# Two raw V buffers and three transposed buffers, another attention order, and another tail in a one-core attention and soft-MoE kernel

## The chip, the cores and the metric

The kernel runs on one core of a Trainium2 chip. The metric is the device time of one execution in microseconds (us); the time given for a kernel is the median of several runs. Engine names are those of the profile: PE (matrix multiply), DVE (VectorE), ACT (ScalarE), POOL (GpSimd) and SP (here only an issuer of transfers).

## What is computed

Four batches of eight heads, 768 tokens, head size 64: attention to the last 96 tokens and to 8 global keys, with a linear bias by distance. Its output, as 3072 tokens of 512 values, goes through a soft mixture of 8 experts with 4 slots each. All is float32.

```python
scores = 1.0 / np.sqrt(D) * np.matmul(q, k.transpose(0, 1, 3, 2)) + bias     # bias = -slope(head) * distance
scores = np.where(is_global | is_local, scores, -1000000000.0)
a = np.exp(scores - np.max(scores, axis=-1, keepdims=True))
attn_out = np.matmul(a / (np.sum(a, axis=-1, keepdims=True) + 1e-09), v)
x = np.ascontiguousarray(attn_out.transpose(0, 2, 1, 3)).reshape(B * S, H * D)
logits = x @ phi
d = np.exp(logits - logits.max(0, keepdims=True)); d /= d.sum(0, keepdims=True) + 1e-09
slot_input = (d.T @ x).reshape(E, S_per_e, D)
for e in range(E):
    slot_out[e] = np.maximum(slot_input[e] @ w1[e], 0.0) @ w2[e]             # w1 512x1024, w2 1024x512
c = np.exp(logits - logits.max(1, keepdims=True)); c /= c.sum(1, keepdims=True) + 1e-09
return c @ slot_out.reshape(n_slots, D)
```

## The kernel before

**The order is written out by hand.** `ORDER` (line 58) is a list of some 800 steps such as `('v_lo', 8)` or `('proj', 2, 0, 0)`. The loop at L1069 calls the function of each step (table `steps`, L1055 to L1067), and each function appends its instructions to the engines it names. An engine runs its own instructions strictly in that order and waits where an operand is not there; so the list decides on every engine, and on the transfer queue of SP, what stands behind what. Nothing reorders it.

**Attention.** The work is cut in 16 units, a unit being one batch and a pair of heads. Unit u takes `load_qk` and `load_v` (SP, L421 to L425), `scores` (PE, L556), `biased` (DVE, L565: bias added, running maximum), `max_t`/`max_r`, `exponential` (ACT, L581), `w_hi` (ACT, L584: the float16 upper part of the weights), `w_lo` (L591: the rest, six parts for a unit, on POOL, or on DVE as `w_lo_dve`), `v_hi` (POOL, L524) or `v_hi_act` (ACT, L527) and `v_lo` (DVE, L534), which split the raw V in the same way, `values` (PE, L608), `ev_sums`/`ev_recs`/`ev_mul` (DVE, L621 to L633: the division by the sum). Then `tr` (PE, L645) transposes the outcome into a buffer `xt0` or `xt1`, copied there by `tr_copy` (ACT, L650) or `tr_copy_dve` (DVE, L654), and `logits` (PE, L675) multiplies it by phi. After every fourth unit `logits_all` (DVE, L692) closes a batch. The raw V of all units but a few early ones goes through one buffer `vt`: `load_v` of a unit can only be executed when `v_lo` of the one before has read it.

**Memory for weights.** The weights are 64 units of 0.5 MB. 52 of them have a place in the tile `mem` (`HELD`), whose end is at first taken by the attention's buffers (`BUFFERS`); `ld` (L415, SP) loads them in pairs (`PAIRS`) or singly as places come free. The other 12 (`late`, L419) overwrite units that the first expert layer has used up.

**The tail.** After the last unit, a chain over the softmax of the experts ends in `dispatch`, `add` (L769), `slots` (L853); `hid` (L877, PE) is the first expert layer in 8 blocks of 16 matmuls, `relu`/`relu_dve` (L882, L885) its activation, `htp`/`htc` (L890) transposes it, `proj` (L904, PE) is the second layer for four column blocks n, `osc`, `spread` (L913) and `sot` rearrange it, and `comb(n, b)` (L965, PE) gives the output of block n for batches b and b+1 in four banks. `outc`/`outl` (DVE L789, ACT L792) copy these out, and `out` (`out_dma`, L975) has SP issue the transfer to memory. The softmax over slots that `comb` needs is made by `cmax`, `csub`, `cexp`, `csum`, `crec`, `cmul` (L926 to L942), batch by batch.

**The flag.** The fast path holds only for inputs within certain limits. `chk_*` steps gather the evidence, `set_flag` (L1009) turns it into a number and `write_flag` (L1012) stores it; L1076 loads it on every engine, L1077 branches over the general path that stands behind it in the program, and then the engines meet at the end of the program (L1288). In `ORDER` `write_flag` stands behind the last copies, and the loads of L1076 behind the last `out`.

Of the kernel before, what the change touches and what calls it, by code (L numbers as in the profile page):

```python
# [26 lines left out]
NJ = 7  # L27
# [25 lines left out]
PAIRS = 12  # L53
SPLIT = (40, 48)
LATE_AT = (0, 2, 4, 6, 16, 18, 20, 22, 1, 3, 5, 7)
BUFFERS = (("tab0", TABW), ("tab1", TABW), ("raw0", S + KW), ("tab2", TABW), ("raw1", S + KW), ("tab3", TABW), ("tb1", 2 * TW), ("tb2", 2 * TW),
           ("v0", 904), ("vt", NJ * 2 * D), ("xn2", XH), ("tb0", 2 * TW), ("ph1", PW), ("ph0", PW), ("v1", 904), ("xt0", S), ("xt1", S), ("xn0", XH), ("xn1", XH))
# [255 lines left out]
def tile_attention_moe(ctx: ExitStack, tc: tile.TileContext, qk, v, phi, w1, w2, nn, out):  # L313
# [46 lines left out]
    by_head = "p (j i d) -> p j i d"  # L360
    first = 20 * UNIT
    early_q = {2: mem[:, first:first + S + KW], 3: mem[:, first + S + KW:first + 2 * (S + KW)]}
    first += 2 * (S + KW)
    early_v = {1: mem[:, 19 * UNIT:19 * UNIT + VC], 2: mem[:, first:first + VC], 3: mem[:, first + VC:first + 2 * VC]}

    def rqs(u):
        return early_q.get(u, rq[u % 2])

    def vraws(u):
        return early_v.get(u, buf("vt")).rearrange(by_head, j=NJ, i=2)  # L370

    vhi = [buf(f"v{i}", VH).bitcast(F16).rearrange(by_head, j=NJ, i=2) for i in range(2)]
    vlo = [buf(f"v{i}", VV)[:, VH:VV].bitcast(F16).rearrange(by_head, j=NJ, i=2) for i in range(2)]
    tabs = [buf(f"tab{p}").bitcast(BF16).rearrange("p (i c) -> p i c", i=2) for p in range(NP)]
    tbuf = [buf(f"tb{k}").rearrange("p (i c) -> p i c", i=2) for k in range(3)]
    PH = PW // 2
    phi_ = [buf(f"ph{i}", PH).bitcast(F16) for i in range(2)]
    plo_ = [buf(f"ph{i}")[:, PH:2 * PH].bitcast(F16) for i in range(2)]
    xnb = [buf(f"xn{k}")[0:KB].rearrange("p (t f) -> p t f", t=NJ) for k in range(3)]
    xtb = [buf("xt0"), buf("xt1")]  # L380
    table_space = mem[:, area["xn0"][0]:area["xn1"][1]]


# [264 lines left out]
    def tr_copy(u, k):  # L648
        a, n = ((0, 4 * KB), (4 * KB, S - 4 * KB))[k]
        nc.scalar.copy(out=xtb[u % 2][:, a:a + n], in_=ms.pop((u, k))[:, 0:n])  # L650

    def tr_copy_dve(u, k):
        a, n = ((0, 4 * KB), (4 * KB, S - 4 * KB))[k]
        nc.vector.tensor_copy(out=xtb[u % 2][:, a:a + n], in_=ms.pop((u, k))[:, 0:n])  # L654
# [17 lines left out]
    def logits_of(u, k):  # L672
        for s in range(4):
            n = min(SW, S - SW * s)
            nc.tensor.matmul(out=ms[u][32 * s:32 * s + 32, 0:n], lhsT=phis[:, units[u - k][1], :], rhs=xtb[(u - k) % 2][:, SW * s:SW * s + n],  # L675
                             start=(k == 1), stop=(k == 0), skip_group_check=True)
# [296 lines left out]
    def out_dma(n, b, s):  # L973
        o = obs[n, b, s]
        nc.sync.dma_start(out=out_rows(out, n, b)[:, OUT_COLS[s]:OUT_COLS[s] + o.shape[1]], in_=o)  # L975
# [76 lines left out]
    def table_pair(p):  # L1052
# [19 lines left out]
    last_banks.close()
# [219 lines left out]
```

## Time and profile before

| | |
|---|---|
| runs | 193.59, 194.54, 196.99 us; median 194.54 us |
| profiled execution | 192.0 us, of which the profile's span is 190.1 us |
| PE, DVE, ACT, POOL busy in the span | 172.3, 143.1, 124.7, 100.4 us |
| data moved | 61.43 MB at a mean of 323 GB/s |
| attention, until the last `ev_mul` | to 127.9 us |
| chain from there to the first matmul of `hid` | to 136.45 us |
| `hid` | 136.45 to 150.39 us |
| `htp`, `proj`, `comb` | 150.3 to 181.03 us |
| last copies, last transfers, branch, meeting of the engines | 181.03 to 190.1 us |

A row of the profile gives an engine and line, its operation, the operand written and read, and how often (x). Busy time is time in which an instruction of an engine is executed; idle time is put down to the instruction or transfer that released the engine. A name such as `mem` covers many buffers, since most of them are pieces of that one tile.

### The profile page before, as it was taken

How to read it: one execution, taken by the hardware profiler on the slowest of the kernel's cores; microseconds unless marked ns; L12 is line 12 of the kernel's file. 1: busy time of each engine (PE TensorE's matmuls, PEld its weight loads, DVE VectorE, ACT ScalarE, POOL GpSimd, SP SyncE). 2: the span in 40 equal slices, each digit the busy share in tenths (PEclk: the TensorE clock that was granted, in tenths of full speed). 3: DMA queues.
4: the chain of work that ended last, by engine and by line, in shares of the span. 5: the costliest groups of instructions: out<-in, count | busy, mean ns of one | idle time of the engine just before them, and what ended most of it. 6: DMA issues, size and time to landing. Idle time of an engine off the chain costs nothing. (4 is left out here: it accounts for less than half of the span.)

```text
span 190.1 us, 7005 instructions
## 1 busy us (share of the span) xinstructions
PE 172.3 (91%) x2923; PEld 129.9 (68%) x2923; DVE 143.1 (75%) x396; ACT 124.7 (66%) x163; POOL 100.4 (53%) x139
## 2 busy tenths in 40 slices
PE   8999999999799998999999998899999999899800
PEld 2567898989688786878779896584533477687700
DVE  5899899998979979899999999998910612554230
ACT  3399999997989988989699999934200002124420
POOL 6716978987847779768899867802104010000000
PEclk9999999999999999999999999999999999999995
DMA  6999998988997997988548898999999998567872
GB/s 211 415 420 414 423 410 323 403 295 272 393 390 253 335 393 206 385 320 251 179 154 314 299 326 292 340 337 406 414 400 411 407 400 350 193 228 293 313 280 76
DMA packets 16027, 61.43 MB, mean 323 GB/s; under 512 B 1778, under 2 KB 4082, under 8 KB 14450
## 3 DMA queue, kind: packets, MB, share of 16 engines
q1 hardware_dynamic: 15984, 60.89, 85.9%
q8 instruction: 25, 0.41, 0.9%
q14 instruction: 16, 0.13, 0.2%
q10 hardware_dynamic: 2, 0.00, 0.0%
HBM read 54.59 MB, written 6.29 MB: 320 GB/s over the span
## 5 line engine op out<-in xcount | busy, mean ns | idle before, releaser
L591 POOL TENSOR_TENSOR mem<-mem 128x432 f16<-128x432 f32 x81 | 85.9, 1092 | 24.0 <-ACT mem L584 18.1
L556 PE MATMUL sc<-mem 64*128 64x216 f32 (+2 forms) x448 | 45.6, 338 | 2.6 <-DMA mem<-in_qk_dram 1.4
L581 ACT ACTIVATE mem<-mem,nb 128x1296 f32<-128x1296 f32 x32 | 43.5, 1376 | 1.4 <-DVE rsall L621 0.8
L608 PEld LDWEIGHTS <-mem 128*128 128x128 f16 x1248 | 41.6, 97 | 3.1 <-issue 1.6
L608 PE MATMUL x<-mem 128*128 128x65 f16 (+1 forms) x1248 | 43.3, 193 | 0.3 <-POOL mem L591 0.2
L556 PEld LDWEIGHTS sc<-mem 64*128 64x128 f32 x448 | 37.0, 186 | 9.1 <-DVE mx L565 4.1
L584 ACT CAST mem<-mem 128x1296 f16<-128x1296 f32 x31 | 39.5, 1273 | 4.8 <-PE x L608 4.1
L565 DVE CUSTOM_DVE_ANT_1 mem<-sc,mem,mx 128x864 f32<-128x864 f32 x32 | 35.6, 1111 | 1.3 <-DVE mx L565 0.3
L633 DVE CUSTOM_DVE_ANT_1 mem<-x,rc 120x448 f32<-120x448 f32 x32 | 18.8, 621 | 0.5
L534 DVE SCALAR_TENSOR_TENSOR mem<-mem 128x896 f16<-128x896 f32 x16 | 17.5, 1091 | 2.0 <-POOL mem L524 1.3
L645 PE MATMUL m<-ident,mem 120*128 120x120 f32 x105 | 16.3, 277 | 2.1 <-ACT mem L650 1.0
L904 PE MATMUL x<-mem 128*32 128x128 f32 x512 | 16.9, 275 | 1.2 <-issue 0.9
L565 DVE CUSTOM_DVE_ANT_1 mem<-sc,mem 128x864 f32<-128x864 f32 x16 | 16.8, 1052 | 0.9 <-POOL mem L591 0.8
L904 PEld LDWEIGHTS x<-mem 128*32 128x32 f32 x512 | 13.4, 109 | 4.2 <-issue 2.8
L645 PEld LDWEIGHTS m<-ident,mem 120*128 120x128 f32 x105 | 10.8, 141 | 5.5 <-ACT mem L650 1.6
L789 DVE COPY mem<-l 128x480 f32<-128x480 f32 (+1 forms) x14 | 7.6, 593 | 8.5 <-PE l L965 8.5
L877 PE MATMUL l<-mem,sl 128*32 128x512 f32 x128 | 13.9, 593 | 0.0
L792 ACT COPY mem<-m 128x128 f32<-128x128 f32 (+1 forms) x7 | 1.8, 265 | 17.3 <-PE m L890 12.1
L527 ACT ACTIVATE mem<-mem 128x896 f16<-128x896 f32 x13 | 12.3, 947 | 0.8 <-DMA mem<-in_v_dram 0.7
L792 ACT COPY mem<-l 128x480 f32<-128x480 f32 x12 | 6.3, 563 | 9.4 <-PE l L965 9.4
L650 ACT COPY mem<-m 128x288 f32<-128x288 f32 (+1 forms) x25 | 11.5, 470 | 0.7 <-PE m L645 0.6
L885 DVE TENSOR_SCALAR mem<-l,zr 128x512 f32<-128x512 f32 x4 | 2.8, 748 | 10.3 <-PE l L877 10.3
(164 smaller groups left out, 188.2 us busy)
## 6 DMA issues: line engine op xcount, KB each, us to landing
mem<-in_w_dram SPq DMA_DIRECT2D x38, 512.0 KB, 8.7
mem<-in_qk_dram SPq DMA_DIRECT2D x16, 832.0 KB, 6.4
mem<-in_w_dram SPq DMA_DIRECT2D x12, 1024.0 KB, 8.8
mem<-in_v_dram SPq DMA_DIRECT2D x16, 448.0 KB, 5.4
out_dram<-mem SPq DMA_DIRECT2D x16, 240.0 KB, 2.5
out_dram<-mem SPq DMA_DIRECT2D x8, 288.0 KB, 4.1
mem<-in_w_dram SPq DMA_DIRECT2D x2, 256.0 KB, 7.9
mem<-in_w_dram SPq DMA_DIRECT2D x1, 300.0 KB, 6.3
```

Of the source, the lines that this page charges most:

```text
L527: nc.scalar.activation(out=vhi[u % 2][:, :, :, 0:D], in_=vraws(u), func=AF.Copy, scale=V_SC)
L534: nc.vector.scalar_tensor_tensor(out=vlo[k].rearrange("p j i d -> p (j i) d"), in0=vraws(u).rearrange("p j i d -> p (j i) d"), scalar=V_SC ...
L556: nc.tensor.matmul(out=z[:, i, at:at + n], lhsT=r_[r, KCOL[j]:KCOL[j] + KR], rhs=r_[r, KW + KB * j:KW + KB * j + n], start=True, stop=True)
L565: nc.vector.tensor_tensor_reduce(out=tb(u)[:, :, BW * k:BW * k + BW], in0=sc[(3 * u + k) % 2][:, :, 0:BW], in1=table.unit(u % NP, k), scal ...
L581: nc.scalar.activation(out=t, in_=t, func=AF.Exp, bias=nbs[u], scale=T_SC)
L584: nc.scalar.copy(out=blocks(phi_[i])[:, :, 0:QW], in_=tb(u)[:, i].rearrange("p (s c) -> p s c", c=QW))
L591: (engine or nc.gpsimd).tensor_tensor(out=blocks(plo_[i])[:, c, 0:QW], in0=tb(u)[:, i].rearrange("p (s c) -> p s c", c=QW)[:, c], in1=bloc ...
L608: nc.tensor.matmul(out=x[:, (D + 1) * t:(D + 1) * t + d], lhsT=w[:, c:c + P], rhs=vv[:, j, i, 0:d], start=(z == 0), stop=(z == len(ops) - ...
L633: nc.vector.tensor_tensor_reduce(out=xnb[(u // 2) % 3][:, :, c:c + D], in0=xv[:, i, :, 0:D], in1=rcs.pop((u, i)).unsqueeze(2).to_broadcast ...
L645: nc.tensor.transpose(out=m[:, at:at + KB], in_=xnb[(u // 2) % 3][:, t, P * (p % 2):P * (p % 2) + P], identity=ident[0:KB, 0:KB])
L877: nc.tensor.matmul(out=mo["h", a][n][32 * s:32 * s + 32, :], lhsT=slv(a, c, s), rhs=wu[0, 4 * a + s, c][:, 512 * n:512 * n + 512], start=( ...
L904: nc.tensor.matmul(out=xx[32 * s:32 * s + 32, n % 2, 0:w], lhsT=hts[a][c // 4][:, c % 4, s], rhs=wu[1, 4 * a + s, n][:, w * c:w * c + w], ...
```

## The change

Between the buffers, `vt` becomes `vt0` and `vt1` (chosen by the unit's parity) and `xt0`, `xt1` become `xt0`, `xt1`, `xt2` (chosen by the unit modulo 3). The buffers together grow by 1664 floats per partition (0.85 MB), so they begin at unit 23.8 of `mem` where they began at 25.4; `PAIRS` goes from 12 to 11, and two half loads (`SPLIT`) go. A step `out_act` is added, which is `out` issued by ACT, and `ORDER` is written anew.

```diff
-PAIRS = 12
-SPLIT = (40, 48)
+PAIRS = 11
+SPLIT = ()
...
-           ("v0", 904), ("vt", NJ * 2 * D), ("xn2", XH), ("tb0", 2 * TW), ("ph1", PW), ("ph0", PW), ("v1", 904), ("xt0", S), ("xt1", S), ("xn0", XH), ("xn1", XH))
+           ("v0", 904), ("vt1", NJ * 2 * D), ("xn2", XH), ("tb0", 2 * TW), ("ph1", PW), ("ph0", PW), ("v1", 904), ("xt1", S), ("xt2", S), ("xt0", S), ("xn0", XH), ("xn1", XH))
...
     def vraws(u):
-        return early_v.get(u, buf("vt")).rearrange(by_head, j=NJ, i=2)
+        return early_v.get(u, buf(f"vt{u % 2}")).rearrange(by_head, j=NJ, i=2)
...
-    xtb = [buf("xt0"), buf("xt1")]
+    xtb = [buf(f"xt{k}") for k in range(3)]
...
-        nc.scalar.copy(out=xtb[u % 2][:, a:a + n], in_=ms.pop((u, k))[:, 0:n])
+        nc.scalar.copy(out=xtb[u % 3][:, a:a + n], in_=ms.pop((u, k))[:, 0:n])
...
-    def out_dma(n, b, s):
+    def out_(e, n, b, s):
         o = obs[n, b, s]
-        nc.sync.dma_start(out=out_rows(out, n, b)[:, OUT_COLS[s]:OUT_COLS[s] + o.shape[1]], in_=o)
+        e.dma_start(out=out_rows(out, n, b)[:, OUT_COLS[s]:OUT_COLS[s] + o.shape[1]], in_=o)
+
+    out_dma, out_act = (lambda *a: out_(nc.sync, *a)), (lambda *a: out_(nc.scalar, *a))
```

Counted over the new list: three parts of `w_lo` move from POOL to DVE (81 and 15 become 78 and 18), one `v_hi` of POOL becomes a `v_hi_act` (unit 8), two `tr_copy` of ACT become `tr_copy_dve`, one `csub` and one `cmul` go from DVE to POOL, two of four `relu_dve` become `relu`, and of the last copies (`outc`, `outl`) three net go from DVE to ACT. `hid` blocks stand in the order (0,0), (0,1), (1,0), (0,2), (1,1), (0,3), (1,2), and (1,3) only behind the first `htp` and `proj`; before they alternated between expert halves 0 and 1. Of the softmax over slots, `csum(0)`, which stood in the chain ahead of `hid`, stands behind its start. In SP's queue, 27 units of weights stand ahead of the last `scores`, where there were 29.

**Place 1, DVE, around the close of batch 0.** L692 is `logits_all(3)`; the two L565 ISA rows are `biased` of two heads (the one on `sc_151` is unit 7's, that on `sc_150` unit 8's), L633 is `ev_mul`, L654 a `tr_copy_dve`. Before:

```order
L633 ISA mem,xmax<-x,rc 120x7x64
L633 ISA xmax 120x1
L565 ISA mem,mx<-sc_151,mem,mx 128x2x432
L565 ISA mx 128x1
L692 ISA lsb,al<-m,lsb 96x240
L692 ISA al 96x1
L692 ISA lsb,al<-m,lsb 32x48
L692 ISA al 32x1
L565 ISA mem,mx<-sc_150,mem 128x2x432
L565 ISA mx 128x1
```

After:

```order
L654 COPY mem<-m 128x480
L633 ISA mem,xmax<-x,rc 120x7x64
L633 ISA xmax 120x1
L565 ISA mem,mx<-sc_151,mem,mx 128x2x432
L565 ISA mx 128x1
L565 ISA mem,mx<-sc_150,mem 128x2x432
L565 ISA mx 128x1
L692 ISA lsb,al<-m,lsb 96x240
L692 ISA al 96x1
L692 ISA lsb,al<-m,lsb 32x48
L692 ISA al 32x1
```

A `biased` stands ahead of `logits_all(3)` now, and a copy that ACT made stands here.

**Place 2, POOL, from its first split of V to its last part of the weights.** L524 is `v_hi`, L591 `w_lo`, L978 (L980 in the changed file) a check. Before:

```order
L479 COPY perm<-ident 128x128
L524 TENSOR_SCALAR mem<-mem 128x14x64 x2
L591 TENSOR_TENSOR mem<-mem 128x2x216 x41
L524 TENSOR_SCALAR mem<-mem 128x14x64
L591 TENSOR_TENSOR mem<-mem 128x2x216 x23
L978 COPY fl<-nv 128x1
```

After:

```order
L479 COPY perm<-ident 128x128
L524 TENSOR_SCALAR mem<-mem 128x14x64 x2
L591 TENSOR_TENSOR mem<-mem 128x2x216 x78
L929 TENSOR_TENSOR lnat<-lnat,cst 120x256
L942 TENSOR_TENSOR lnat<-lnat,cst 120x256
L980 COPY fl<-nv 128x1
```

The third `v_hi` of POOL, that of unit 8, is gone from between its parts of the weights, and so is the check.

**Place 3, the end of SP's queue and of PE.** L975 is `out`, the TENSOR_LOAD is the load of the flag, the two ISA rows turn it into the branch's condition. SP before:

```order
L975 DMA out_dram<-mem 128x480 x4
L975 DMA out_dram<-mem 128x576 x2
L975 DMA out_dram<-mem 128x480 x4
L975 DMA out_dram<-mem 128x576 x2
L1076 TENSOR_LOAD flag
L1076 ISA x2
L1077 COMPARE_AND_BRANCH
```

SP after:

```order
L975 DMA out_dram<-mem 128x480 x2
L975 DMA out_dram<-mem 128x576 x2
L975 DMA out_dram<-mem 128x480 x2
L1078 TENSOR_LOAD flag
L1078 ISA x2
L975 DMA out_dram<-mem 128x480 x2
L975 DMA out_dram<-mem 128x576 x2
L1079 COMPARE_AND_BRANCH
```

The flag's load has moved ahead of SP's last four transfers; the other two of the last six, (3,2,0) and (3,2,1), stand at the end of ACT's queue behind its last copies, ahead of its own flag load. `write_flag` stands on DVE ahead of the four copies of `comb(3, *)` that DVE makes. On PE, L904 x32 is `proj(3,1,1)` before and `proj(3,1)` in one piece after, L965 `comb`, L913 `spread`. PE before:

```order
L965 MATMUL l<-lnat,mem 128x240 x3
L965 MATMUL m<-lnat,mem 128x48
L904 MATMUL x<-mem 32x128 x32
L1006 MATMUL m<-const-float32-1.0,fl_91 1x1
L913 MATMUL m<-mem,perm 128x128
L965 MATMUL l<-lnat,mem 128x240 x3
```

PE after:

```order
L904 MATMUL x<-mem 32x128 x32
L965 MATMUL l<-lnat,mem 128x240 x3
L965 MATMUL m<-lnat,mem 128x48
L965 MATMUL l<-lnat,mem 128x240 x3
L965 MATMUL m<-lnat,mem 128x48
L913 MATMUL m<-mem,perm 128x128
L1008 MATMUL m<-const-float32-1.0,fl_91 1x1
L965 MATMUL l<-lnat,mem 128x240 x3
```

`comb(2,2)` has moved from ahead of the last `proj` to between it and its `spread`.

## Rows read from the trace of the kernel before

**Rows 1.** Windows: length, busy PE, PEld, DVE, ACT, POOL (instructions), clock, DMA share, GB/s.
```profile
20.00:60.00 40.00, 38.06 (x680) 33.52 (x677) 36.84 (x100) 38.11 (x42) 32.19 (x32) 1.00 0.93 351
60.00:100.00 40.00, 38.48 (x702) 31.69 (x701) 37.18 (x93) 36.11 (x43) 32.41 (x31) 1.00 0.80 281
100.00:120.00 20.00, 19.36 (x386) 16.86 (x384) 19.34 (x54) 19.33 (x27) 15.54 (x18) 1.00 0.91 307
136.00:150.00 14.00, 14.00 (x133) 4.47 (x132) 3.90 (x15) 0.42 (x1) 1.98 (x4) 1.00 1.03 407
183.00:185.00 2.00, 0.00 (x0) 0.00 (x0) 0.00 (x0) 0.00 (x0) 0.00 (x0) 1.00 1.03 365
```
**Rows 2.** Timeline of DVE: start, duration, line, operands, idle time before and its releaser.
```profile
20.88 1.06 DVE L565 CUSTOM_DVE_ANT_1 mem<-sc,mem 128x864 f32<-128x864 f32 x1 [0.84 <-POOL mem L591]
...
46.67 1.09 DVE L534 SCALAR_TENSOR_TENSOR mem<-mem 128x896 f16<-128x896 f32 x1 [0.53 <-ACT mem L527]
...
53.49 0.41 DVE L692 CUSTOM_DVE_ANT_0 lsb<-m,lsb 96x240 f32<-96x240 f32 x1 [0.89 <-PE m L675]
...
70.25 1.09 DVE L534 SCALAR_TENSOR_TENSOR mem<-mem 128x896 f16<-128x896 f32 x1 [1.32 <-POOL mem L524]
```
**Rows 3.** Lines of DVE and of ACT, 16 to 126 us: busy, mean ns | idle before.
```profile
L591 DVE TENSOR_TENSOR mem<-mem 128x432 f16<-128x432 f32 x15 | 10.5, 717 | 0.0
...
L654 DVE COPY mem<-m 128x480 f32<-128x480 f32 (+1 forms) x5 | 2.8, 571 | 0.2 <-PE m L645 0.2
...
L527 ACT ACTIVATE mem<-mem 128x896 f16<-128x896 f32 x13 | 12.3, 947 | 0.8 <-DMA mem<-in_v_dram 0.7
L650 ACT COPY mem<-m 128x288 f32<-128x288 f32 (+1 forms) x23 | 10.6, 469 | 0.7 <-PE m L645 0.6
```
**Rows 4.** Timeline of POOL behind its `v_hi` of unit 8.
```profile
70.25 1.96 POOL L591 TENSOR_TENSOR mem<-mem 128x432 f16<-128x432 f32 x1
```
**Rows 5.** Line L591: durations in ns min/median/max, first and last start.
```profile
L591 POOL TENSOR_TENSOR mem<-mem x81: 994/1009/1958, 15.1 to 122.9; 128x432 f16<-128x432 f32 x81
...
L591 DVE TENSOR_TENSOR mem<-mem x15: 596/611/1452, 16.9 to 124.3; 128x432 f16<-128x432 f32 x15
```
**Rows 6.** Timeline of all engines in the chain ahead of `hid`.
```profile
134.59 0.41 DVE L935 TENSOR_REDUCE cst<-lnat 120x8 f32<-120x256 f32 x1
134.92 0.86 DVE L769 SCALAR_TENSOR_TENSOR sacc<-sacc,al,l 128x256 f32<-128x256 f32 x2
```
**Rows 7.** Timeline of PE in the second expert layer.
```profile
151.67 1.08 PE L904 MATMUL x<-mem 128*32 128x128 f32 x32 [0.25 <-ACT mem L792]
...
165.12 1.08 PE L904 MATMUL x<-mem 128*32 128x128 f32 x32
...
178.29 0.49 PE L913 MATMUL m<-mem,perm 128*128 128x128 f32 x2 [0.38 <-ACT mem L792]
179.13 1.90 PE L965 MATMUL l<-lnat,mem 32*128 32x240 f32 x32 [0.35 <-ACT mem L792]
```
**Rows 8.** Line L419, the late weights: issues, then time from issue to landing.
```profile
L419 SPq DMA_DIRECT2D mem<-in_w_dram x12: 327/328/432, 138.4 to 153.6; - x12
...
DMA to landing us min/median/max: 7.8/10.3/10.4
```
**Rows 9.** The end: timeline of DVE, then lines L975, L1076 and L1077 on their queues.
```profile
180.30 2.12 DVE L789 COPY mem<-l 128x480 f32<-128x480 f32 x5 [1.57 <-PE l L965]
...
L975 SPq DMA_DIRECT2D out_dram<-mem x24: 332/344/501, 161.9 to 183.6; - x24
...
DMA to landing us min/median/max: 2.0/2.7/5.2
...
L1076 SPq TENSOR_LOAD <-flag x1: 998/998/998, 184.0 to 184.0; - x1
...
L1077 SPq EVENT_SEMAPHORE  x8: 17/17/17, 188.2 to 188.7; - x8
...
L1077 PEldq COMPARE_BRANCH  x1: 5117/5117/5117, 183.3 to 183.3; - x1
```

More of the change, by code (lines that the diff above doesn't have):

```diff
@@ L360, in tile_attention_moe @@
     by_head = "p (j i d) -> p j i d"
-    first = 20 * UNIT
+    first = 18 * UNIT
     early_q = {2: mem[:, first:first + S + KW], 3: mem[:, first + S + KW:first + 2 * (S + KW)]}
     first += 2 * (S + KW)
-    early_v = {1: mem[:, 19 * UNIT:19 * UNIT + VC], 2: mem[:, first:first + VC], 3: mem[:, first + VC:first + 2 * VC]}
+    early_v = {2: mem[:, first:first + VC], 3: mem[:, first + VC:first + 2 * VC]}
     def rqs(u):
@@ L649, in tr_copy @@
         a, n = ((0, 4 * KB), (4 * KB, S - 4 * KB))[k]
-        nc.scalar.copy(out=xtb[u % 2][:, a:a + n], in_=ms.pop((u, k))[:, 0:n])
+        nc.scalar.copy(out=xtb[u % 3][:, a:a + n], in_=ms.pop((u, k))[:, 0:n])
     def tr_copy_dve(u, k):
         a, n = ((0, 4 * KB), (4 * KB, S - 4 * KB))[k]
-        nc.vector.tensor_copy(out=xtb[u % 2][:, a:a + n], in_=ms.pop((u, k))[:, 0:n])
+        nc.vector.tensor_copy(out=xtb[u % 3][:, a:a + n], in_=ms.pop((u, k))[:, 0:n])
     als, dns = {}, {}
@@ L674, in logits_of @@
             n = min(SW, S - SW * s)
-            nc.tensor.matmul(out=ms[u][32 * s:32 * s + 32, 0:n], lhsT=phis[:, units[u - k][1], :], rhs=xtb[(u - k) % 2][:, SW * s:SW * s + n],
+            nc.tensor.matmul(out=ms[u][32 * s:32 * s + 32, 0:n], lhsT=phis[:, units[u - k][1], :], rhs=xtb[(u - k) % 3][:, SW * s:SW * s + n],
                              start=(k == 1), stop=(k == 0), skip_group_check=True)
@@ L1065, in tile_attention_moe @@
                  turned_act=turned_act, turned_dve=turned_dve, comb=comb, outc_act=outc_act, outc_dve=outc_dve, outl_act=outl_act, outl_dve=outl_dve,
-                 out=out_dma, chk_n=chk_n, chk_l=chk_l, chk_rs=chk_rs, chk_x=chk_x, chk_xr=chk_xr, chk_c=chk_c, chk_all=chk_all,
+                 out=out_dma, out_act=out_act, chk_n=chk_n, chk_l=chk_l, chk_rs=chk_rs, chk_x=chk_x, chk_xr=chk_xr, chk_c=chk_c, chk_all=chk_all,
                  chk_sum=chk_sum, set_flag=set_flag, write_flag=write_flag)
```

4 lines of the change are left out of this document (2 added, 2 removed).

## The prediction

> **What bounds the kernel now.** I began with the busy time by windows, because an average over the span mixes stages with different limits. From 20 to 120 us, the attention, the windows read PE 95.90, DVE 93.36 and ACT 93.55 us busy of 100 (sums of three rows), at a full clock [rows 1]. Three engines work in a circle: PE's scores feed DVE, DVE feeds ACT, ACT feeds POOL and PE again. DVE has 6.64 us idle there, ACT 6.45 and PE 4.10. So in this stage no single wait is the bound, and the most that a better order could give is some of those few microseconds. From 136 to 150 us PE is busy 14.00 of 14.00, and the transfers run at a share of 1.03 and 407 GB/s [rows 1]: there the first expert layer is bound by PE, and no other engine's order can shorten it.
>
> Then I took DVE's timeline and looked for idle time. Four stalls are larger than half a microsecond: 0.84 us at 20.88 for a part of `w_lo` from POOL, 0.53 at 46.67 for ACT's `v_hi_act` (itself late by its V transfer: ACT idled for that transfer 0.7 us [rows 3]), 0.89 at 53.49 for PE's logits ahead of `logits_all(3)`, and 1.32 at 70.25 for POOL's `v_hi` [rows 2]. Together they are 3.58 us, over half of DVE's idle time.
>
> Last, the end. PE's `proj` runs with hardly a gap from 151.67 us; two gaps, 0.38 and 0.35 us, stand around the last `spread` [rows 7]. The last copies begin at 180.30 and take 2.12 us on DVE. The last of the 24 transfers is issued at 183.6 us and the longest takes 5.2 us, so 188.8 us for the last landing, which agrees with SP's semaphores from 188.2 to 188.7. Beside that runs a second chain: PE's branch begins at 183.3 and takes 5.117 us, to 188.4 [rows 9]. Both have to shrink before the end moves; the 1.4 us from 188.7 to the span's end at 190.1 is the engines' meeting.
>
> **The change, part by part.**
>
> *Attention: DVE's work.* Three more `w_lo` parts at a mean of 0.717 us and two more copies at 0.571 us [rows 3] make 2.15 + 1.14 = 3.29 us added. Against it, each of the four stalls loses its cause in the new order: the `w_lo` part that DVE waited for is its own; the load of unit 5's V stands far earlier, as it has a second buffer to go to; a `biased` stands between PE's logits and `logits_all(3)` (place 1), covering 0.89 with 1.05 us of work; and POOL's `v_hi` is ACT's (place 2). That is up to 3.58 us back. DVE's balance: 3.29 - 3.58 = -0.3, about nothing. Bounds: if all four close and the new work falls into the remaining idle time (6.64 - 3.58 = 3.06), the gain is nearly 3.6 us; if as much idle time opens elsewhere as closes, +3.3 us. I take 0, the middle, because the order of eight hundred steps was rewritten and rows of before cannot show where the new stalls lie.
>
> *Attention: the others.* ACT gets one `v_hi_act` (0.947) and loses two copies (2 x 0.469) [rows 3]: 0.0. POOL loses three parts at 1.009 us [rows 5] and a `v_hi`; as it has idle time (40 - 32.19 from 20 to 60 us [rows 1]), that is worth nothing on its own. The third transposed buffer lets a copy be made before PE has read the last but one; as no row shows a copy waiting for that, 0, with the bounds above covering it.
>
> *DVE and POOL at the same time.* POOL's median for a part is 1.009 us, but 1.96 us for the part that began at 70.25, the very moment `v_lo` began on DVE [rows 2, 4]; and DVE's own parts run from 0.611 at the median to 1.452 us [rows 5]. So the two hold each other up. Work moved from POOL to DVE could be paid at 1.45 us instead of 0.72: 3 x 0.735 = +2.2 us; that is a rival below. The Trainium skill ("SBUF — State Buffer", section "Who interferes with whom") says that DVE and GpSimd share one port pair as an exclusive lock, so the later of two fully blocks. By it, a part on DVE beside one on POOL waits its turn; the trace agrees with it in the one long part named, and as most DVE parts sit at the median, it does not agree that each part pays.
>
> *Ahead of `hid`.* `csum(0)`, 0.41 us at 134.59, delays `add` by 0.33 us (134.92 less 134.59) [rows 6]. It goes behind the start of `hid`, where DVE is busy 3.90 of 14 us [rows 1]. -0.3 us; bounds -0.35 and 0 (two strip sums stand closer to the chain and could take its place).
>
> *`hid` and `proj`.* The blocks of half 0 end earlier, so their `relu` and `htp` run beside the last matmuls of half 1; the wait of 0.25 us at 151.67 [rows 7] goes. -0.25 us, bounds -0.5 and 0.
>
> *Weights.* The buffers take 0.85 MB more, so up to that much more waits behind the first layer. At 407 GB/s [rows 1] it is 2.1 us. Before, the last `late` unit is issued at 153.6 and lands 10.3 us later, 163.9 [rows 8]; after, between 163.9 and 166.0. The last in the new queue is wanted only by the block n = 3. The one before it, `ld` 38, is wanted by `proj(2,0)`, which begins at 165.12 [rows 7], 0.55 earlier by the sum above: 164.6. It lands one unit, 0.5 MB or 1.3 us, ahead of the last: 162.6 to 164.7. So it costs 0 to 0.1 us, 0 in the sum; but this transfer is a lid on anything gained earlier.
>
> *Last `spread`.* `comb(2,2)` stands between `proj(3,1,1)` and `spread` now (place 3) and covers the 0.38 us wait at 178.29 [rows 7] for ACT's copy. -0.35 us; bounds -0.4 and 0 (0, if its copies on ACT hold up `sot_act`, which the second wait of 0.35 us would then show doubled).
>
> *The exit.* The flag is written ahead of the last copies, so PE no longer waits with its load until 182.5: it can start at its last matmul's end at 181.03 (179.13 and 1.90 [rows 7]). PE's chain moves by up to 1.4 us. On the side of the transfers, six issues no longer stand in one queue: SP issued the last at 183.6, whereas the last copy ended at 182.42 [rows 9]; with two of the six on ACT the last issue comes up to 1.1 us earlier. But the transfers were at a share of 1.03 from 183 to 185 us [rows 1], so an earlier issue partly only waits longer, and SP's flag load of 0.998 us [rows 9] now stands ahead of four of its transfers, covered if the flag is written over a microsecond before the first of them is ready. I take -0.75 us, the middle of -0.3 and -1.2. By the Trainium skill ("DMA: Bandwidth & Descriptors", section "Issuing engines are not separate DMA queues"), issuing from a second engine saves issue time only and no time of the transfers; by it alone the two ACT issues would be worth about 2 x 0.34 = 0.7 us, an estimate from the median issue [rows 9]. No run here shows it yet.
>
> *Sum.* 0 - 0.3 - 0.25 + 0 - 0.35 - 0.75 = -1.65 us. The profiled execution took 192.0 us (span 190.1), so it would take 190.35, span 188.4. The median of the three runs is 194.54, 2.5 us above the profiled execution; taking that distance as the same for both kernels, 192.9 us.
>
> **Rivals.**
>
> *DVE becomes the bound (slower).* The 3.29 us of added work stands in DVE's queue ahead of `biased` and `v_lo`, on which ACT and PE wait. It decides from the point at which the new order leaves as much idle time on DVE as before, 6.6 us from 20 to 120. For it: DVE is 93% busy there. Against it: the named stalls lose their cause. Time: 192.9 + 3.3 = 196.2 us.
>
> *The lock of DVE and POOL.* The three moved parts fall beside POOL's and run 1.45 us: 192.9 + 2.2 = 195.1 us. For it, the 1.96 us part [rows 4]; against it, the median of 0.611 [rows 5].
>
> *The order packs the attention.* The stalls close and the added work falls into idle time: -3.6 us at the start of `hid`. `proj(2,0)` would want its weights at 161.0 (164.6 - 3.6); they land at 162.6 to 164.7 [rows 8] and give 1.6 to 3.7 us back unless transfers also start earlier. At the kinder end 192.9 - 3.6 + 1.6 = 190.9; with earlier loads 189.3.
>
> *The end does not move.* PE's branch or the last landing hold the end where it is: without the 0.75 us, 193.6 us.
>
> **How the numbers follow.** The forecast gets a chance of 0.42, DVE as the bound 0.2, the lock 0.08, the packed attention 0.18, the unmoved end 0.12. The likeliest alone lies between 191.6 and 194.0 us (the bounds of its small terms). The range for 8 in 10 reaches half-way into the packed attention, 189.9, and past the DVE case by half of the spread of the runs shown, 197.2. A measurement of this kernel tells about 2% from no change, 3.9 us: faster is below 190.65, slower above 198.4. Faster holds most of the packed case and a little of the forecast, 0.18. Slower needs DVE as the bound with further stalls, some half of its case, 0.10. Same is the rest, 0.72.
>
> **What would show it.** In DVE's timeline of the changed kernel the four stalls should be gone and idle time from 20 to 120 us near 6 to 7 us, with `hid` starting within 1 us of 136.1. If DVE's idle time falls under 4 us and `hid` starts at 138 or later, DVE is the bound. If DVE's parts of L591 have a mean near 1 us, it is the lock. An idle PE before `proj(2,0)`, released by a transfer, shows the lid. At the end PE's branch should begin at about 181.2 and SP's last semaphores of the branch stand 0.7 us nearer to PE's last matmul. The prediction is wrong if the attention's length moves by more than 2 us either way, because its term was set to nothing between bounds of -3.6 and +3.3.

## The result and the profile after

Over 20 runs of each, in turns on the same chip, the changed kernel took 191.16 us (189.66 to 193.89) and the kernel before 193.97 us (191.80 to 197.15). The ratio of the two is 0.9896, with a 95% interval of 0.9863 to 0.9930: 1.0% faster, about 2.0 us (1.4 to 2.7). By the bound of 2% that is "the same"; clear of noise it is a gain. The forecast was 192.9 us, 1.65 us less. A second set of 12 runs gave 191.12 us and 0.9876 (0.9833 to 0.9920). Some executions of most kernels here are one or more per cent longer than its others; the ratios leave these out, and as the profiles of b_two and a_comb below are such executions, no total is read from them.

The profiled executions differ by less, a span of 190.1 against 189.1 us, as the one of before lay at the lower end of its runs. In five stages, with the second profile of the changed kernel (run a0) beside the first:

| stage (us) | before | after | a0 | change, after (a0) | forecast |
|---|---|---|---|---|---|
| start of the last `exponential` | 120.05 | 118.46 | 118.64 | -1.59 (-1.41) | 0 |
| from there to the first matmul of `hid` | 16.40 | 15.85 | 15.85 | -0.55 (-0.55) | -0.3 |
| from there to `comb(3,0)` | 42.68 | 42.47 | 42.50 | -0.21 (-0.18) | -0.6 |
| from there to the end of the last copy | 3.28 | 3.37 | 3.38 | +0.09 (+0.10) | 0 |
| from there to the end of the span | 7.70 | 8.92 | 8.41 | +1.22 (+0.71) | -0.75 |
| span | 190.11 | 189.07 | 188.78 | -1.04 (-1.33) | -1.65 |

So the forecast of the whole came out, and two of its terms did not: the attention gave what was put at nothing, and the exit took back what was meant as a gain. Two things stay open. The profiles account for 1.0 to 1.3 us of the 2.0 that the runs show; in which stage the rest sits is not shown. And there is only one profile of the kernel before. In it the attention, from the first `exponential` to the last, takes 107.70 us; in the seven profiles with the changed kernel's attention that are compared here (the two above, a_sp, a_late, a_sp_late, a_best and a_best_act) it takes 105.87 to 106.98. So the gain of 1.59 us is known no better than as 0.7 to 1.8. The first and the last `exponential`, before and after (timelines of ACT):

```profile
12.35 1.36 ACT L581 ACTIVATE mem<-mem,nb 128x1296 f32<-128x1296 f32 x1
...
120.05 1.40 ACT L581 ACTIVATE mem<-mem,nb 128x1296 f32<-128x1296 f32 x1
```
```profile
12.37 1.36 ACT L581 ACTIVATE mem<-mem,nb 128x1296 f32<-128x1296 f32 x1
...
118.46 1.39 ACT L581 ACTIVATE mem<-mem,nb 128x1296 f32<-128x1296 f32 x1
```

The attention first. Windows from 16 us to the start of the last `exponential`, in the kernel before and then after (columns as in [rows 1]):

```profile
16.00:120.05 104.05, 99.93 (x1825) 85.77 (x1825) 97.28 (x252) 97.09 (x113) 83.58 (x83) 1.00 0.88 318
```
```profile
16.00:118.46 102.46, 99.94 (x1825) 85.16 (x1821) 98.22 (x258) 97.45 (x112) 78.45 (x77) 1.00 0.88 319
```

PE does the same work, 99.9 us, in 1.59 us less; all of the gain is idle time that is gone. DVE is busy 0.94 us longer and idle 2.53 us less (6.77 to 4.24), which is the same -1.59 by arithmetic. Of the four stalls of [rows 2] two, at 20.88 and 46.67, are gone without a trace. Around `logits_all(3)` 0.66 of 0.89 us stays, now for the scores; where DVE waited 1.32 us for POOL's `v_hi`, it waits 0.77 for the outcome of `values` from PE; and a new stall of 0.83 us stands at 82.86 (timeline of DVE after):

```profile
52.53 1.06 DVE L565 CUSTOM_DVE_ANT_1 mem<-sc,mem 128x864 f32<-128x864 f32 x1 [0.66 <-PE sc L556]
...
70.42 0.17 DVE L621 TENSOR_TENSOR rsall<-x,eps 120x14 f32<-120x14 f32 x1 [0.77 <-PE x L608]
...
82.86 1.06 DVE L565 CUSTOM_DVE_ANT_1 mem<-sc,mem 128x864 f32<-128x864 f32 x1 [0.83 <-POOL mem L591]
```

The lines of DVE from 16 to 126 us and L591 by engine, to be held against [rows 3, 5]: a part of `w_lo` on DVE takes 0.676 us where it took 0.717, and three more parts and two more copies cost 1.3 and 0.8 us.

```profile
L591 DVE TENSOR_TENSOR mem<-mem 128x432 f16<-128x432 f32 x18 | 11.8, 676 | 0.0
...
L654 DVE COPY mem<-m 128x288 f32<-128x288 f32 (+1 forms) x7 | 3.6, 521 | 0.0
```
```profile
L591 POOL TENSOR_TENSOR mem<-mem x78: 998/1011/1803, 15.1 to 121.3; 128x432 f16<-128x432 f32 x78
...
L591 DVE TENSOR_TENSOR mem<-mem x18: 543/604/1202, 16.3 to 122.7; 128x432 f16<-128x432 f32 x18
```

Then the end, by the timeline of PE, and by the lines L975, L1078 and L1079 (L1076 and L1077 before, [rows 9]):

```profile
134.31 1.06 PE L877 MATMUL l<-mem,sl 128*32 128x512 f32 x8
...
162.50 1.08 PE L904 MATMUL x<-mem 128*32 128x128 f32 x32
...
176.78 1.90 PE L965 MATMUL l<-lnat,mem 32*128 32x240 f32 x32 [0.89 <-DVE flag L1014]
```
```profile
L975 SPq DMA_DIRECT2D out_dram<-mem x22: 332/340/2486, 159.4 to 182.3; - x22
...
L975 ACTq DMA_DIRECT2D out_dram<-mem x2: 378/1166/1955, 179.3 to 179.7; - x2
...
L1078 PEldq TENSOR_LOAD <-flag x1: 766/766/766, 177.3 to 177.3; - x1
L1078 SPq TENSOR_LOAD <-flag x1: 744/744/744, 177.4 to 177.4; - x1
...
L1079 SPq EVENT_SEMAPHORE  x8: 17/17/17, 186.6 to 187.6; - x8
...
L1079 PEldq COMPARE_BRANCH  x1: 4587/4587/4587, 178.2 to 178.2; - x1
```

PE's branch runs from 178.2 to 182.8, 5 us earlier than before, where 181.2 was forecast. But one issue on SP takes 2.486 us and one on ACT 1.955, where the longest of all 24 took 0.501 before [rows 9]. They last from 179.2 to 181.7 and from 179.73 to 181.69, within the time of PE's branch (line L975 on SP, 180 to 181 us, and timeline of ACT, after):

```profile
L975 SPq DMA_DIRECT2D out_dram<-mem x1: 2486/2486/2486, 179.2 to 179.2; - x1
```
```profile
179.73 1.96 ACTq L975 DMA_DIRECT2D out_dram<-mem  x1
```

The last copy ends at 180.15, and yet the last issue is at 182.3. From 181 to 182 us, when no issue had begun since 179.73 but one at 181.8, the transfers are at a share of 0.20; once the issues go on they are at 1.05 (windows after):

```profile
181.00:182.00 1.00, 0.00 (x0) 0.00 (x0) 0.00 (x0) 0.00 (x0) 0.00 (x0) 0.50 0.20 64
183.00:185.00 2.00, 0.00 (x0) 0.00 (x0) 0.00 (x0) 0.00 (x0) 0.00 (x0) 0.50 1.05 378
```

### The profile page after: what moved, and what is told of

Its sections match the earlier page's. It is cut to its first block, busy times and chain, and to the rows that moved or that the text cites. A ratio compares the mean times of both kernels' runs of the same rounds, so it can differ in the third digit from the quotient of the medians.

```text
span 189.1 us, 6999 instructions
## 1 busy us (share of the span) xinstructions
PE 170.8 (90%) x2920; PEld 129.7 (69%) x2920; DVE 142.5 (75%) x394; ACT 126.1 (67%) x167; POOL 94.2 (50%) x137
## 4 chain that ended last, share of the span: by engine, by line
PE 41%; DVE 17%; ACT 15%; POOL 11%; issue 7%; DMA 5%; ACTq 0%; DVEq 0%; POOLq 0%
POOL mem L591 9%; PE x L904 9%; PE l L877 7%; PE x L608 6%; DVE mem L565 6%; ACT mem L581 6%; ACT mem L584 5%; DMA mem<-in_qk_dram 5%; PE sc L556 4%; PE l L965 4%; PE m L645 2%; DVE mem L633 2%; DVE mem L534 2%; ACT mem L527 1%; DVE mem L591 1%
## 5 line engine op out<-in xcount | busy, mean ns | idle before, releaser
L591 POOL TENSOR_TENSOR mem<-mem 128x432 f16<-128x432 f32 x78 | 80.4, 1060 | 31.4 <-ACT mem L584 31.4
L565 DVE CUSTOM_DVE_ANT_1 mem<-sc,mem,mx 128x864 f32<-128x864 f32 x32 | 35.5, 1109 | 1.2 <-POOL mem L591 0.2
L633 DVE CUSTOM_DVE_ANT_1 mem<-x,rc 120x448 f32<-120x448 f32 x32 | 18.8, 621 | 0.3
L565 DVE CUSTOM_DVE_ANT_1 mem<-sc,mem 128x864 f32<-128x864 f32 x16 | 16.8, 1053 | 1.6 <-POOL mem L591 0.8
L904 PE MATMUL x<-mem 128*32 128x128 f32 x512 | 17.3, 275 | 0.6 <-issue 0.6
L904 PEld LDWEIGHTS x<-mem 128*32 128x32 f32 x512 | 13.9, 109 | 3.8 <-issue 2.9
L789 DVE COPY mem<-l 128x480 f32<-128x480 f32 (+1 forms) x14 | 8.2, 622 | 8.3 <-PE l L965 8.2
L527 ACT ACTIVATE mem<-mem 128x896 f16<-128x896 f32 x14 | 13.3, 950 | 0.0
L792 ACT COPY mem<-l 128x480 f32<-128x480 f32 (+1 forms) x12 | 6.0, 537 | 10.6 <-PE l L965 10.6
L591 DVE TENSOR_TENSOR mem<-mem 128x432 f16<-128x432 f32 x18 | 11.8, 676 | 0.0
L650 ACT COPY mem<-m 128x480 f32<-128x480 f32 (+1 forms) x23 | 10.9, 477 | 1.3 <-PE m L645 1.2
L882 ACT ACTIVATE mem<-l,zr 128x512 f32<-128x512 f32 x2 | 1.4, 688 | 14.8 <-PE l L877 14.8
```

The lines of the kernel that those rows point to most:

```text
L527: nc.scalar.activation(out=vhi[u % 2][:, :, :, 0:D], in_=vraws(u), func=AF.Copy, scale=V_SC)
L565: nc.vector.tensor_tensor_reduce(out=tb(u)[:, :, BW * k:BW * k + BW], in0=sc[(3 * u + k) % 2][:, :, 0:BW], in1=table.unit(u % NP, k), scal ...
L591: (engine or nc.gpsimd).tensor_tensor(out=blocks(plo_[i])[:, c, 0:QW], in0=tb(u)[:, i].rearrange("p (s c) -> p s c", c=QW)[:, c], in1=bloc ...
L633: nc.vector.tensor_tensor_reduce(out=xnb[(u // 2) % 3][:, :, c:c + D], in0=xv[:, i, :, 0:D], in1=rcs.pop((u, i)).unsqueeze(2).to_broadcast ...
L904: nc.tensor.matmul(out=xx[32 * s:32 * s + 32, n % 2, 0:w], lhsT=hts[a][c // 4][:, c % 4, s], rhs=wu[1, 4 * a + s, n][:, w * c:w * c + w], ...
```

## The exit: flag and issuer, each by itself

Four kernels, the changed one among them (a0, unedited), give the two edits of the exit in all combinations. The theories: F, the early flag sends PE's branch into the last transfers and holds up their issue; Q, two issuing engines hold each other up.

```diff
 a_sp:      -('out_act', 3, 2, 0), ('out_act', 3, 2, 1)
            +('out', 3, 2, 0), ('out', 3, 2, 1)
 a_late:    -('comb', 3, 2), ('write_flag', 0), ('outc_dve', 3, 0, 1)
            +('comb', 3, 2), ('outc_dve', 3, 0, 1)
            ...
            -('outc_dve', 3, 2, 2), ('outc_act', 3, 2, 1)
            +('outc_dve', 3, 2, 2), ('write_flag', 0), ('outc_act', 3, 2, 1)
 a_sp_late: both
```

> The changed kernel itself, as the reference of this set; about 191 us against 193 to 194 for the kernel before. In its profile the two last issues that stand behind one another on SP and on ACT took 2.49 and 1.96 us where the kernel before took at most 0.50 us for an issue. If that belongs to the order of the tail, the issues of over 1.5 us come again; if it was an accident of one execution they do not.

> The changed kernel with all of its last six transfers issued by SP again, flag still written early. Theory F (the branch of PE, begun at 178.2 us, fetches instructions over the same DMA engines in the midst of the last transfers and holds them up): the long issue of about 2 us stays, now on SP alone, last landing within 0.5 us of that of the changed kernel, time within 0.5 us. Theory Q (two engines issue at once and get in each other's way): no issue over 0.6 us, last landing about 1.5 us earlier, time 1 us less.

> The changed kernel with the flag written behind the last copies, as in the kernel before; ACT still issues two of the last six transfers. Theory F: no issue over 0.6 us, the transfers are out about 2 us sooner; PE's branch starts about 2 us later and ends at about 187, so the time is 0 to 1 us less than that of the changed kernel. Theory Q: the long issues stay, and with the later branch the time is 0 to 1 us more.

> Both undone: all issued by SP, flag written behind the last copies, so the tail's end as in the kernel before. Both theories: no issue over 0.6 us, the span ends 7.7 us after the last copy as before, where the changed kernel took 9.0. If the prediction's term for the exit (-0.75 us) was right, it is 0.75 us slower than the changed kernel; by the profiles it is 1.0 us faster.

| | a0 | a_sp | a_late | a_sp_late |
|---|---|---|---|---|
| flag | early | early | late | late |
| issuers of the last six | SP and ACT | SP | SP and ACT | SP |
| longest issue, us | 1.95 | 2.81 | 1.10 | 0.76 |
| last copy to end of span, us | 8.41 | 9.53 | 7.91 | 7.89 |
| time, us (runs) | 191.12 (12) | 191.77 (6) | 191.67 (6) | 190.07 (6) |
| ratio to the kernel before | 0.9876 | 0.9894 | 0.9897 | 0.9810 |
| its interval | 0.983 to 0.992 | 0.982 to 0.997 | 0.982 to 0.998 | 0.974 to 0.988 |

The lines L975 and L1079 of a_sp, then of a_sp_late:

```profile
L975 SPq DMA_DIRECT2D out_dram<-mem x24: 332/347/2814, 159.6 to 184.0; - x24
```
```profile
L975 SPq DMA_DIRECT2D out_dram<-mem x24: 332/348/755, 159.7 to 181.9; - x24
...
L1079 SPq EVENT_SEMAPHORE  x8: 17/17/17, 186.5 to 187.0; - x8
...
L1079 PEldq COMPARE_BRANCH  x1: 4427/4427/4427, 181.0 to 181.0; - x1
```

On the issues of about 2 us F holds and Q falls: with SP alone and an early flag the long issue is still there, 2.814 us, and with a late flag none of that length is left. F's other expectations came out in part: in a_sp the exit is 0.6 to 1.1 us longer than in the two profiles of the changed kernel, where the last landing was to come within 0.5, and no kernel of the four keeps under the 0.6 us that the theories gave to the issue otherwise. The issuers count too: with a late flag the longest issue is 1.10 us with two issuers (1.14 in a_best_act below) and 0.76 with SP alone (0.46 in a_best below). What moved from 178.5 to 181.8 us fits with F (transfers in that window, the changed kernel, then a_sp_late):

```profile
DMA packets 350, 0.63 MB, mean 190 GB/s; under 512 B 45, under 2 KB 346, under 8 KB 346
...
q8 instruction: 2, 0.03, 6.0%
```
```profile
DMA packets 503, 0.86 MB, mean 260 GB/s; under 512 B 63, under 2 KB 502, under 8 KB 502
...
q8 instruction: 1, 0.02, 1.8%
```

In the five profiles with an early flag (these two, the changed kernel's first, a_vt2 and a_pool) the exit takes 8.41 to 9.53 us; with a late flag and SP alone 7.89 and 7.60 (a_best), and 7.70 before; with a late flag and two issuers 7.91 and 8.56 (a_best_act). That the instruction packets of PE's branch are what blocks the issue is argued from their time; shown is that the early flag brings it about. The early flag also brings forward the branches of POOL (177.5 us) and DVE (179.4) and SP's own load of the flag, and no run tells them apart from PE's.

With a late flag, ACT's two issues don't help: the spans of a_late and a_sp_late are equal (188.3 and 188.4 us), but the profiled execution of a_late was the shortest of its six, and the times are 191.67 and 190.07. A second pair stands further below. By time the late flag is shown to gain only with SP alone; a_late can't be told from a0, where F expected it to be faster by 0 to 1 us. The fastest of all is a_sp_late, 0.9810: both edits of the exit undone. The ratios to the kernel before have intervals that overlap; set directly against each other, over the runs that the ratios use, its mean lies 1.3 us below that of a0, with a 95% interval of 0.6 to 1.9. So the changed kernel is faster without the two edits of its exit. The expectation for a_sp_late had this as the reading of the profiles, 1.0 us.

## The attention: where the 1.6 us could come from

**Two stalls alone, in the kernel before (b_two).** `v_hi` of unit 8 on ACT, and a `biased` ahead of `logits_all(3)`; nothing else.

```diff
-('logits_all', 3), ('w_lo', 5, 1, 1), ('biased', 8, 0)
+('biased', 8, 0), ('logits_all', 3), ('w_lo', 5, 1, 1)
...
-('exponential', 8, 0), ('ev_mul', 6, 1), ... ('v_hi', 8)
+('exponential', 8, 0), ('v_hi_act', 8), ('ev_mul', 6, 1), ...
```

> The kernel before with only two of the four stalls' causes removed: the v_hi of unit 8 moves from POOL to ACT, right behind the unit's first exponential, and the first biased of unit 8 stands ahead of logits_all(3). Theory S (the large stalls of DVE were the loss): the stalls of 0.89 us at 53.5 and of 1.32 us at 70.3 go and hid starts 1.0 to 2.2 us earlier than 136.45. Theory C (the circle of engines is bound by the sum of work, and a closed stall opens again at the next place): the two stalls go, others open, and hid starts less than 0.5 us earlier.

194.40 us (10 runs) against 194.03: ratio 0.9997 (0.9940 to 1.0054). Nothing measurable; a gain of more than 1.2 us is ruled out, and with it most of what theory S expected. Where `hid` starts can't be compared, so theory C is borne out by the time alone. A row of the kernel before that the prediction did not use tells why one of the two could give little: what `logits_all(3)` waited for was PE's logits, and these stood behind `scores(8,0)`, which waited 1.39 us for unit 8's q and k (timeline of PE before):

```profile
51.45 1.00 PE L556 MATMUL sc<-mem 64*128 64x216 f32 x8 [1.39 <-DMA mem<-in_qk_dram]
```

The `biased` moved ahead needs those scores too. The same is seen in the changed kernel, where 0.66 of 0.89 us stays. The cause of this stall lay a step further back than the stall. For the other, no row tells why its end gave nothing.

**One raw V buffer in the new order.** The second buffer also takes the V of unit 1, which had an early place of its own before. A first attempt (a_vt) lets units 0 and 1 share the one buffer and lets weights be loaded over it while it is in use, and so does the attempt with two transposed buffers (a_xt) with theirs: what they compute is not what the kernel computes, and they have waits for weights that belong to the edit alone (217.12 and 203.31 us). They tell nothing of the buffers but that this order also reuses their space early.

> The changed kernel with one raw V buffer for both parities; each load of V from unit 5 on is issued where the one before has been read, as in the kernel before. Theory V (the second buffer frees the transfer queue and the units' V): ACT waits for V again, hid starts 1 us or more later than 134.5 us, towards 136.4. Theory O (the gain of the attention comes from the order on the engines, V came in time for nearly all units anyway): hid starts within 0.4 us of 134.5.

> The changed kernel with two transposed buffers used in turn; only one copy (unit 2, second part) has to move behind the logits of unit 1 for it. The prediction put the third buffer at 0: hid starts within 0.3 us of 134.5 us, time the same within 0.5 us. The rival, that the third buffer carries part of the gain: hid starts 0.5 us or more later.

So the third transposed buffer is left untested. In the order, only one copy (unit 2, second part) stands ahead of the last reader of the buffer it would have shared. The mended form of the other:

```diff
-        return early_v.get(u, buf(f"vt{u % 2}"))
+        return early_v.get(u, buf("vt0" if u in (0, 4) else "vt1"))
 and in ORDER, for u = 6 to 15: ('load_v', u) moved to behind ('v_lo', u - 1)
```

> The changed kernel with one raw V buffer from unit 5 on (units 0 and 4 keep the other); each later load of V is issued where the V before it has been read for the last time, some 10 to 33 steps ahead of the unit's v_hi_act, where the changed kernel leaves 24 to 61 and the kernel before left 21 to 30. Theory V (the second buffer takes waits for V out of the attention): ACT waits for V transfers on several units, and hid starts 1 to 6 us later than 134.5 us. Theory O (the order on the engines alone): hid within 0.4 us of 134.5.

197.93 us (4 runs), ratio 1.0256 (1.0179 to 1.0332), 7 us more than the changed kernel; `hid` starts at 142.46, later than theory V's own 1 to 6 us. ACT waits for V on five units, 8.0 us in all, which is about the 8 us by which `hid` is late; 5.14 us of it is one wait (timeline of ACT, then line L527, of a_vt2):

```profile
60.91 0.95 ACT L527 ACTIVATE mem<-mem 128x896 f16<-128x896 f32 x1 [5.14 <-DMA mem<-in_v_dram]
```
```profile
L527 ACT ACTIVATE mem<-mem x14: 935/950/972, 22.9 to 125.0; 128x896 f16<-128x896 f32 x14
...
  DMA mem<-in_v_dram: 8.0, 5
```

In the changed kernel ACT waits for V nowhere, in the kernel before once, 0.7 us [rows 3]. The long wait has a second cost: behind it PE stood idle from 61 to 64 us, and from 64 to 70 its granted clock is 0.50, the lower of its two levels (1.2 GHz). From 16 us to the last `exponential` PE is busy 102.61 us instead of 99.94 (windows of a_vt2):

```profile
61.00:64.00 3.00, 0.00 (x0) 0.00 (x0) 0.94 (x2) 3.00 (x3) 0.90 (x1) 0.92 0.91 344
64.00:67.00 3.00, 2.12 (x30) 2.07 (x31) 3.00 (x6) 3.00 (x5) 1.44 (x2) 0.50 0.11 44
```

Theory V holds for this order: with the loads of V placed as here, it loses more without the second buffer than it gained with it. Whether another place for the loads would do with one buffer was not tried. Nor does it say that the buffer would speed up the old order; the old order waited only 0.7 us for V.

**Three parts of `w_lo` back on POOL (a_pool).**

```diff
-('w_lo_dve', 8, 0, 2), ('w_lo_dve', 9, 1, 2), ('w_lo_dve', 10, 0, 1)
+('w_lo', 8, 0, 2), ('w_lo', 9, 1, 2), ('w_lo', 10, 0, 1)
```

> The changed kernel with three of DVE's parts of w_lo given back to POOL (unit 8 head 0 part 2, unit 9 head 1 part 2, unit 10 head 0 part 1), so 81 on POOL as in the kernel before. If DVE bounds the attention, hid starts up to 2.0 us earlier (3 x 0.676). If POOL's parts then come late for values, hid starts 0.3 to 1.5 us later. If the lock of the two engines paid for the moves, POOL's mean for a part rises or falls by more than 0.05 from 1.060 us.

191.42 us (4 runs), ratio 0.9873 (0.9769 to 0.9976), not to be told from the changed kernel's. From the first `exponential` to the last it takes 107.28 us, 0.3 more than the longest of the seven profiles with the changed kernel's attention. DVE's waits for POOL grew from 0.83 us to two, 1.88 and 0.90 (timeline of DVE in a_pool):

```profile
82.91 1.06 DVE L565 CUSTOM_DVE_ANT_1 mem<-sc,mem 128x864 f32<-128x864 f32 x1 [1.88 <-POOL mem L591]
...
92.36 1.06 DVE L565 CUSTOM_DVE_ANT_1 mem<-sc,mem 128x864 f32<-128x864 f32 x1 [0.90 <-POOL mem L591]
```

DVE saved three parts (its parts take 9.3 us in all instead of 11.8) and waited 1.95 us longer for POOL's. So taking work from DVE did not shorten the circle of engines. POOL's mean for a part is 1.062 us, against 1.060 in the changed kernel, so no lock was paid for the move.

## The tail: `comb(2,2)`

`comb(2,2)` ahead of `proj(3,1,1)` again, and `set_flag` behind that block's copies (a_comb); the same with a late flag and SP alone (a_best), or with a late flag and ACT's two issues (a_best_act).

```diff
-('proj', 3, 1, 1), ... ('comb', 2, 2), ('osc_act', 3), ... ('set_flag', 0), ('outc_dve', 2, 2, 0)
+('comb', 2, 2), ('proj', 3, 1, 1), ... ('osc_act', 3), ... ('outc_dve', 2, 2, 0), ('set_flag', 0)
```

> The changed kernel with comb(2,2) ahead of proj(3,1,1) again, as in the kernel before, and set_flag behind the copies of that block on DVE so that it does not hold them up. The prediction's term (comb(2,2) behind the last proj covers a wait: -0.35 us) would make this 0.35 us slower up to the start of comb(3,0). The profile of the changed kernel says otherwise: there comb(3,0) waits 0.89 us for the copies of comb(2,2), more than the 0.38 and 0.35 us of the kernel before, so comb(3,0) starts 0.15 us earlier here, or the same.

> Both ends of the tail undone: comb(2,2) and set_flag as in the run above, all last transfers issued by SP, flag written behind the last copies. Against about 191.1 us for the changed kernel, 1.0 us less for the exit (as both undone gave) and 0.15 less for comb: about 189.9 us, ratio to the kernel before 0.980.

> As the run above, but ACT issues two of the last six transfers, flag still late. If the issue from a second engine costs or gives nothing, the same within 0.4 us and no issue over 1.1 us. If two issuers get in each other's way, 0.5 to 1.5 us more, as the times of the two runs with a late flag (191.67 and 190.07) say; their spans, 188.3 and 188.4, say the same time.

| | a_comb | a_best | a_best_act |
|---|---|---|---|
| time, us (12 runs each) | 191.76 | 191.20 | 192.48 |
| ratio to the kernel before | 0.9934 | 0.9911 | 0.9975 |
| its interval | 0.9896 to 0.9973 | 0.9874 to 0.9948 | 0.9933 to 1.0016 |
| `hid` to `comb(3,0)`, us (42.47 after) | 43.31 | 43.41 | 43.45 |

All three miss what I expected: undoing the reorder does not give 0.15 us, it costs 0.84 to 0.98 us between `hid` and `comb(3,0)`. In time, a_comb can't be told from the changed kernel. The timeline of PE in a_best shows a part of the loss:

```profile
177.26 0.49 PE L913 MATMUL m<-mem,perm 128*128 128x128 f32 x2 [0.39 <-ACT mem L792]
...
178.57 1.69 PE L965 MATMUL l<-lnat,mem 32*128 32x240 f32 x29 [0.70 <-ACT mem L792]
```

Both waits are there, 1.09 us against the 0.89 of the changed kernel, because the new order has ACT copy a block of `comb(2,2)` ahead of `sot_act` and another behind it, and `comb(3,0)` waits for them. The larger part shows as no idle time of PE: `comb(2,2)` itself takes 1.52 us, from 174.28 to 175.80, where the changed kernel takes 1.01 (174.20 to 175.21). After its first matmuls PE passes a semaphore at 174.7, just as DVE ends its second copy of `comb(2,0)`, 1.22 us behind 173.45 (timeline of all engines of a_best):

```profile
173.45 1.22 DVE L789 COPY mem<-l 128x480 f32<-128x480 f32 x2 [1.75 <-PE l L965]
...
174.28 0.97 PE L965 MATMUL l<-lnat,mem 32*128 32x240 f32 x5
...
175.80 1.08 PE L904 MATMUL x<-mem 128*32 128x128 f32 x32
```

So `comb(2,2)` waited for a copy of the block before it, with only one `proj` between the two; that it was a bank which that copy had to free is argued from the time. So a_best, meant to be the best, loses by the one edit what it gains by the other. Of the late flag with two issuers, the second pair says as the first did: 192.48 against 191.20 us. Set directly against each other, a_best_act is slower by 1.3 us (95% interval 0.7 to 1.9). So beside a late flag ACT's issues cost 1.3 to 1.6 us in both pairs; what does it is not shown.

## Why the prediction was right, and where it was not

**What bounds the attention** was right: the same PE work, the same three engines near the limit, and a gain that consists of idle time alone. The signs that were to show it came in part: DVE is idle 4.27 us from 20 to 120 us, not 6 to 7, and `hid` starts 1.8 us ahead of 136.1, not within 1 us of it.

**Attention, the term of 0** was mis-sized: -1.59 us, inside its bounds of -3.6 and +3.3. The step that failed is the added work, put at 3.29 us by the means of the old rows, as if each added microsecond made DVE busy that much longer. Up to the last `exponential` the parts took 1.4 us more, the copies 0.8, and two short reductions came into the stretch with 0.8 (the parts, before and then after, 16 us to the last `exponential`):

```profile
L591 DVE TENSOR_TENSOR mem<-mem 128x432 f16<-128x432 f32 x12 | 8.3, 704 | 0.0
```
```profile
L591 DVE TENSOR_TENSOR mem<-mem 128x432 f16<-128x432 f32 x15 | 9.7, 665 | 0.0
```

Yet DVE's busy time grew by only 0.94 us. Its records overlap their neighbours: the busy times of its lines there sum to 113.4 us in 97.28 of the engine before, and to 116.2 in 98.22 after. The other half, the stalls, was sized at 3.58 us and measured as 2.53 us of idle time. I took the middle of the bounds for want of a row; the two halves did not cancel. Nor does DVE's balance say what made the stretch shorter, since a_pool took work from DVE and gained nothing; which steps of the order did it is not shown.

**The lock and DVE as the bound** fell, by the profile and by a_pool. **The packed attention** came true in part. Its lid was near: `ld` 38, the second-last weight in the queue, was issued at 151.5 and landed 10.5 us later, at 162.0, and `proj(2,0)` began at 162.50 with no wait for a transfer (line L415 after, 151.2 to 151.7 us):

```profile
L415 SPq DMA_DIRECT2D mem<-in_w_dram x1: 327/327/327, 151.5 to 151.5; - x1
...
DMA to landing us min/median/max: 10.5/10.5/10.5
```

A start of `hid` earlier by more than half a microsecond would have met it, unless this load also came earlier; the landing of 162.6 to 164.7 in the prediction was a little late.

**Ahead of `hid`** -0.55 us for -0.3: `csum(0)` is gone from ahead of `add`, as argued; of the rest no experiment tells. **`hid` to `comb(3,0)`** -0.21 for -0.6: the waits of 0.25 and 0.38 us are gone as said [rows 7], but the last one grew from 0.35 to 0.89 us, for DVE's copy of `comb(2,2)`, which now comes behind the last `proj`. The row above names the flag's write, which follows that copy on DVE; with the flag written late the wait is the same, and the copy is named (timeline of PE in a_late):

```profile
177.01 1.90 PE L965 MATMUL l<-lnat,mem 32*128 32x240 f32 x32 [0.90 <-DVE mem L789]
```

The prediction named a risk at this place and priced it at 0.35, but for ACT's copies ahead of `sot_act`; it was DVE's.

**The exit** is the term whose argument failed: -0.75 was forecast, +1.22 and +0.71 measured. PE's branch did start earlier, as the argument had it. What the argument left out is that the branch was not alone in its time: the early flag put it among the last transfers and their issue stalled. "The last issue comes up to 1.1 us earlier" is not true of the change: it begins 2.1 us behind the end of the last copy, where it was 1.2 before. It is true of two issuers with a late flag, where it begins 0.4 us behind (a_late, 180.8 and 180.39); but the exit is 7.91 us there and no shorter than the 7.70 before, as the prediction's own reserve had it, that an earlier issue partly only waits longer. A row that could have warned was there: before, the branch began at 183.3 us, when only one of the 24 issues was still to begin.

Two misses of opposite sign made the sum right, which was luck. Read by stages, the gain lies in the attention, by its order with the second V buffer, and not in the tail.

Some of the prediction's figures don't come out of its own terms. The small terms' bounds add up to 192.1 to 194.2 us, not 191.6 to 194.0; half of the spread of the three runs is 1.7 us, so the upper end would be 197.9 and not 197.2; and 3.29 us of work does not quite fit into 3.06 us of idle time. None of it touches the sum.

## What to carry to other kernels

Before work is pulled forward at the end of a program, look at what else is in flight there: here an earlier flag, and with it earlier branches, held up the last transfers, whose landing the program waits for. A stall is closed where its cause lies, not where it shows: two named stalls of 2.2 us gave nothing measurable by themselves, a whole new order gave 0.7 to 1.8 us. And an order that leads with its loads needs the buffers for it; a buffer's worth can't be told from the stalls of an order written without it.

## What was not expected of the hardware

The issue of an output transfer, 0.33 to 0.50 us in the kernel before, took up to 2.8 us on SP and 2.1 us on ACT while PE's branch was under way. PE's branch itself took 4.3 to 5.9 us in the profiles here, where SP's took 0.05. And the same attention, instruction for instruction, started `hid` at 134.31 to 134.65 us in five profiles and at 135.16 and 135.72 in two others (a_best, a_best_act); in the last the first `exponential` already began at 14.01 us, where the others began at 11.99 to 12.37. So a difference of half a microsecond between two single profiles says little there.
